# A decode block on one core: two heads a unit in three fixed 64 KB slots, without the tile framework

## The chip, the cores and the metric

The kernel runs on one core of one Trainium2 chip. The metric is the device time of one execution in microseconds (us). The kernel before was timed in three runs: 1331.37, 1329.55 and 1329.38 us, median 1329.55 us. Beside the timed runs, one execution was recorded by the hardware profiler; all rows quoted here come from that one.

The names of the engines: PE is TensorE (PEld its weight loads), DVE is VectorE, ACT is ScalarE, POOL is GpSimd, SP is the sequencer that issues nearly all DMA transfers. DMA stands for the core's 16 DMA engines, which share every large transfer.

## What is computed

One decode step of a transformer block for a batch of 2 rows, all in float32. The attention part has 32 heads with a cache of 8192 positions and 128 elements a head; the feed-forward part has 1792 hidden columns.

```python
# B, D = 2, 512;  H, Sk, Dh = 32, 8192, 128;  F = 1792
q = (layernorm(x) @ wq).reshape(B, 1, H, Dh)               # one query per row and head
scores = einsum("bhqd,bhkd->bhqk", q, k_cache) * Dh ** -0.5
p = softmax(scores)
o = einsum("bhqk,bhkd->bhqd", p, v_cache)
h = x + o.reshape(B, 1, H * Dh) @ wo
g = silu(layernorm(h) @ w_gate)
out = h + (g * (layernorm(h) @ w_up)) @ w_down
```

Each of the two caches has 64 pieces (2 rows x 32 heads) of 8192 x 128 floats, 4 MB a piece. Keys and values are 537 MB together, the five weight matrices 28 MB more. Every byte is used once, so all of it passes from HBM to SBUF once.

## The kernel before

The function `tile_decode_block` is written on the tile framework, with the order of the instructions given by hand (`manual_schedule`). Its unit of work is one (head, row) pair `i`, 64 of them. A piece of 4 MB lies in SBUF as 128 partitions x 32 KB: 64 positions of 128 elements on each partition.

**The ring.** All that is streamed (keys, values, wq and wo in four pieces of 2 MB each, w_gate, w_up, w_down) goes through one ring of five slots of 32 KB a partition (`RING = 5`, line 15; the pool on line 51). A list `order` (lines 80 to 99), made once, sets the order of the transfers: keys run ahead of values by up to four pairs (`LEAD`, `after`, lines 74 to 78). `pump()` (line 136) issues the next transfer on SP's queue as soon as the fifth item before it is marked used. The queue is one, so a transfer that waits for its slot holds all that stand behind it.

**The scores** (DVE). For each pair, `mult` (line 226) multiplies the keys in place by the query, which stands on every partition, and `reduce` (line 229) sums each position's 128 products. Both go in halves of 4096 elements a partition. `local_max` (line 237) takes each partition's maximum; a matmul against the identity (line 241) turns these 128 numbers into a row, DVE takes the row's maximum (line 245), and a matmul (line 247) spreads it to all partitions. ACT takes the exponentials with their sums (line 252), a matmul adds the sums up (line 256), DVE takes the reciprocal (line 260).

**The values** (PE). `pv` (line 262) makes 64 matmuls a pair: the weights are one column of the exponentials, the moving operand 128 positions' values of one column `j`, 128 columns wide. Four of PE's column groups are used in turn (`t = j % 4`), which puts four partial sums on partitions 0, 32, 64 and 96 of `opart`. `epilogue` (line 277) adds them up and divides.

**The projections.** `project_q` (line 197) has the query already copied to all partitions as its weights (128 columns wide), so its 16 matmuls for eight heads give a query that stands on all 128 partitions. It runs four times, before each group of eight heads. `project_o` (line 286) does the same grouping for wo. After the last value, lines 364 to 426 do the second layernorm, the gate and up projections (line 375), the transposes (line 394), the down projection (lines 406 and 421) with 512 columns, and the output.

## Time and profile before

| what | us |
|---|---|
| median of three runs | 1329.55 |
| span of the profiled execution | 1330.2 |
| DVE busy | 1156.7 |
| PE busy | 599.8 |
| ACT busy | 80.8 |

The span runs from the first instruction to the last on the slowest core (here the only one). No separate time is recorded for the profiled execution; its span is 0.65 us above the median of the timed runs. To read the page: "busy" is the time in which an engine has an instruction in work. The DMA share is the mean busy share of the 16 DMA engines, GB/s what they moved. The chain of waits starts at the last instruction and goes back at each step to what released it. PEclk is the clock that TensorE was granted, as a part of full speed: it moves between 0.50 and 1.00 in this trace.

### The profile page before, as it was taken

What the parts mean: (1) busy time and instruction counts of PE and PEld (TensorE: products, weight loads), DVE (VectorE), ACT (ScalarE), POOL (GpSimd) and SP (SyncE); (2) the same over time, 40 slices, a digit from 0 to 9 for tenths busy, and PEclk for the clock granted to TensorE, in tenths of its full rate; (3) what the DMA queues carried; (4) which work ended last, traced back from release to release, by engine and by line L of the source; (5) the groups of instructions that cost most, each with busy time, mean ns of one, the idle gap of its engine ahead of it and who ended that gap; (6) DMA issues with size and microseconds to landing.
All of it is one profiled execution on the core that took longest, in us unless ns stands there. A gap on an engine that the chain in (4) does not pass through costs nothing.

```text
span 1330.2 us, 19346 instructions
## 1 busy us (share of the span) xinstructions
PE 599.8 (45%) x9004; PEld 379.0 (28%) x9004; DVE 1156.7 (87%) x478; ACT 80.8 (6%) x341; POOL 1.9 (0%) x9
## 2 busy tenths in 40 slices
PE   5443432247443324425652443442644544244586
PEld 2322322134232213323321332232332223222341
DVE  6999999997899999988889999997799999999501
ACT  1000000001000000000100000000100000000010
POOL 0000000000000000000000000000000000000000
PEclk9656666568666666667776656665766875666687
DMA  9999999999999999999999999999999999999996
GB/s 410 425 440 426 432 433 430 431 433 435 428 430 434 429 437 429 433 432 431 433 428 429 437 428 438 427 428 437 425 438 392 428 436 427 437 429 437 428 417 266
DMA packets 28680, 565.91 MB, mean 425 GB/s; under 512 B 2484, under 2 KB 2484, under 8 KB 11448
## 3 DMA queue, kind: packets, MB, share of 16 engines
q1 hardware_dynamic: 28596, 564.67, 99.0%
q8 instruction: 70, 1.15, 0.3%
q14 instruction: 10, 0.08, 0.0%
q10 hardware_dynamic: 4, 0.00, 0.0%
HBM read 564.66 MB, written 0.00 MB: 425 GB/s over the span
## 4 chain that ended last, share of the span: by engine, by line
DMA 47%; DVE 45%; PE 7%; issue 0%; ACT 0%; SPq 0%; DVEq 0%; ACTq 0%
DMA ring<-in_A_k_cache_dram 34%; DVE s L229 22%; DVE ring L226 22%; DMA ring<-in_A_v_cache_dram 12%; PE wide L204 4%; PE opart L267 2%; DMA ring<-in_B_w_up_dram 1%; DMA ring<-in_A_wq_dram 1%; DVE m L237 0%; PE wide L406 0%; DVE r L260 0%; DVE gm L245 0%; PE small L241 0%; PE wide L375 0%; PE small L401 0%
## 5 line engine op out<-in xcount | busy, mean ns | idle before, releaser
L226 DVE TENSOR_TENSOR ring<-ring,qsb 128x4096 f32<-128x4096 f32 (+1 forms) x130 | 565.5, 4350 | 76.3 <-DMA ring<-in_A_k_cache_dram 61.5
L229 DVE TENSOR_REDUCE s<-ring 128x32 f32<-128x4096 f32 (+1 forms) x130 | 565.1, 4347 | 0.4 <-DVE gm L245 0.3
L267 PE MATMUL opart<-ring,p 128*1 128x128 f32 x8192 | 358.6, 357 | 120.4 <-DMA ring<-in_A_v_cache_dram 120.4
L267 PEld LDWEIGHTS opart<-ring,p 128*1 128x1 f32 x8192 | 250.4, 108 | 214.8 <-DMA ring<-in_A_v_cache_dram 125.4
L241 PE MATMUL small<-ident,m 128*1 128x128 f32 x128 | 31.1, 335 | 277.1 <-DVE m L237 277.1
L247 PE MATMUL small<-gm,nscale 1*128 1x1 f32 x128 | 35.8, 346 | 264.4 <-DVE gm L245 264.4
L247 PEld LDWEIGHTS small<-gm,nscale 1*128 1x128 f32 x128 | 30.3, 292 | 274.3 <-DVE gm L245 272.5
L241 PEld LDWEIGHTS small<-ident,m 128*1 128x1 f32 x128 | 5.5, 81 | 296.8 <-DVE m L237 294.5
L204 PE MATMUL wide<-ring,xb 128*128 128x512 f32 x128 | 58.6, 618 | 3.0 <-DMA ring<-in_A_wq_dram 3.0
L256 PE MATMUL small<-rs,ones 128*128 128x1 f32 x128 | 36.2, 352 | 46.9 <-ACT p L252 46.9
L245 DVE TENSOR_REDUCE gm<-small 1x1 f32<-1x128 f32 x64 | 17.4, 272 | 35.8 <-PE small L241 35.8
L280 ACT ACTIVATE osb<-opart 128x128 f32<-128x128 f32 x64 | 17.7, 277 | 494.4 <-PE opart L267 494.4
L256 PEld LDWEIGHTS small<-rs,ones 128*128 128x128 f32 x128 | 30.7, 298 | 52.4 <-ACT p L252 52.4
L204 PEld LDWEIGHTS wide<-ring,xb 128*128 128x128 f32 x128 | 25.0, 198 | 34.1 <-issue 34.1
L249 ACT ACTIVATE nb<-small 128x1 f32<-128x1 f32 x64 | 10.9, 171 | 375.1 <-PE small L247 374.7
L290 PE MATMUL attn<-ring,oT 128*2 128x512 f32 x64 | 33.0, 672 | 0.3 <-ACT oT L283 0.3
L282 PE MATMUL small<-r,osb 128*128 128x1 f32 x128 | 31.2, 313 | 4.2 <-ACT osb L280 4.2
L282 PEld LDWEIGHTS small<-r,osb 128*128 128x128 f32 x128 | 25.8, 251 | 24.9 <-issue 18.1
L283 ACT ACTIVATE oT<-small 128x1 f32<-128x1 f32 x64 | 11.0, 171 | 259.9 <-PE small L282 259.9
L365 DVE TENSOR_TENSOR h<-attn,xs 2x512 f32<-2x512 f32 x1 | 0.7, 679 | 29.0 <-PE attn L290 29.0
L252 ACT ACTIVATE p<-s,nb 128x64 f32<-128x64 f32 x64 | 22.3, 348 | 2.1
L237 DVE TENSOR_REDUCE m<-s 128x1 f32<-128x64 f32 x64 | 14.1, 220 | 2.2
(51 smaller groups left out, 79.4 us busy)
## 6 DMA issues: line engine op xcount, KB each, us to landing
ring<-in_A_k_cache_dram SPq DMA_DIRECT2D x63, 4096.0 KB, 32.0
ring<-in_A_v_cache_dram SPq DMA_DIRECT2D x63, 4096.0 KB, 30.6
ring<-in_A_wq_dram SPq DMA_DIRECT2D x4, 2048.0 KB, 25.6
ring<-in_A_wo_dram SPq DMA_DIRECT2D x4, 2048.0 KB, 28.3
ring<-in_A_k_cache_dram SPq DMA_DIRECT2D x4, 1024.0 KB, 11.1
ring<-in_A_v_cache_dram SPq DMA_DIRECT2D x4, 1024.0 KB, 24.9
ring<-in_B_w_gate_dram SPq DMA_DIRECT2D x4, 896.0 KB, 25.9
ring<-in_B_w_up_dram SPq DMA_DIRECT2D x4, 896.0 KB, 17.5
```

What stands on the lines that cost most here:

```text
L204: nc.tensor.matmul(ps, xb[:, c * B + b, :], w[:, c, n : n + 512], start=(c == 0), stop=(c == DC - 1),)
L226: nc.vector.tensor_tensor(kt, kt, qb, op=OP.mult)
L229: nc.vector.tensor_reduce(st[i]["s"][:, j0 : j0 + n], k_view(i, j0, n), axis=AX.X, op=OP.add)
L241: nc.tensor.matmul(st[i]["mrow"], st[i]["m"], ident, start=True, stop=True)
L245: nc.vector.tensor_reduce(gm, st[i]["mrow"], axis=AX.X, op=OP.max)
L247: nc.tensor.matmul(nb_ps, nscale, gm, start=True, stop=True)
L252: nc.scalar.activation(st[i]["p"], st[i]["s"], AF.Exp, bias=nb, scale=SCALE, accum_out=rs)
L256: nc.tensor.matmul(st[i]["den"], ones, rs, start=True, stop=True)
L267: nc.tensor.matmul(o[32 * t : 32 * t + 1, :], st[i]["p"][:, j : j + 1], vt[:, j, :], start=(j < 4), stop=(j >= NJ - 4),)
L280: nc.scalar.activation(osb, opart[i % 2], AF.Copy)
L282: nc.tensor.matmul(ot_ps, osb, st[i]["r"], start=True, stop=True)
L290: nc.tensor.matmul(attn, oT[:, h, :], w[:, h - g * G, :], start=(h == 0), stop=(h == H - 1))
```

## The change

The kernel is written anew without the tile framework: `decode_block` places every tensor at a fixed address and orders the engines by semaphores that it counts itself (`Count`, `take`). What it computes is the same. Its parts:

- **Units.** A unit is two neighbouring heads of one row; there are 32. Partitions 0 to 63 hold the first head, 64 to 127 the second, and each partition holds 128 positions (64 KB, one contiguous run in HBM). DVE's two large instructions cover a whole unit, 16384 elements a partition.
- **Slots.** Three slots of 64 KB a partition: A and B for keys in turn, C for values. wq is loaded whole (8 MB) into C before the first values, wo whole into A after the last keys there, w_gate and w_up into B, w_down into C.
- **Order on SP's queue.** After wq and the keys of units 0 and 1, values of unit u and keys of unit u + 2 alternate. Values wait until PE has finished the values before them (`s_pv`), keys until DVE has summed the keys that lie in their slot (`s_red`).
- **Values.** 32 matmuls a unit: the weights are 8 columns (4 positions x 2 heads, each head's column zero on the other head's partitions), the moving operand 512 columns. Only the matching blocks of the result are used: ACT copies all of it with the factor 1/sum, and four small matmuls (`gather`) pick out and add up the blocks.
- **The loop.** PE's work of units 0 to 30 is one loop (`Fori`) with one unit as its body: values(u), gather(u), softmax(u + 1). The other engines' instructions are unrolled.
- **Projections.** The query is projected in rows (32 weight columns, four column groups), then copied to the 64 partitions of its head by 32 small matmuls. wo's heads 0 to 29 go in four column groups, heads 30 and 31 after the last values. In the down projection the output is held in four groups of 128 columns on partitions 0, 32, 64 and 96 (`f4`), 13 of 14 row blocks go in two halves of 256 columns, and the result leaves in two DMAs.
- **Layouts.** wo and w_down come from the host arranged by partition; wq, w_gate and w_up are read with four neighbouring rows on a partition. So each transfer reads one contiguous run of 2 to 64 KB for each partition, where wo and w_down were read in runs of 2 KB before, and wq in runs of 4 KB.

```diff
-    ring = ctx.enter_context(tc.tile_pool(name="ring", bufs=RING))
...
+    A, BB, C = (BASE + s * SLOT for s in range(3))
+    ks = [arena("kA", A, [P, NJ, DH]), arena("kB", BB, [P, NJ, DH])]
+    vs = arena("vC", C, [P, NJ, DH])
+    wq_s = arena("wqC", C, [P, DC, H * DH])
+    wo_s = arena("woA", A, [P, H, D])
...
+    load(s["kB"], flat(ks[1], 0, NJ), kv_src(k_cache, 1))
+    for u in range(NU - 1):
+        if u == 0:
+            sp.wait_ge(s["pe"].h, 3)
+        else:
+            sp.wait_ge(s["pv"].h, u)
+        load(s["v"], flat(vs, 0, NJ), kv_src(v_cache, u))
+        if u + 2 < NU:
+            sp.wait_ge(s["red"].h, u + 1)
+            load(s["kB" if u % 2 else "kA"], flat(ks[u % 2], 0, NJ), kv_src(k_cache, u + 2))
+    sp.wait_ge(s["red"].h, NU - 1)
+    load(s["wo"], wo_s[:, :, :], wo)
+    sp.wait_ge(s["pv"].h, NU - 1)
+    cut = 96
+    load(s["v"], flat(vs, 0, cut), kv_src(v_cache, NU - 1)[:, : cut * DH])
+    load(s["v2"], flat(vs, cut, NJ), kv_src(v_cache, NU - 1)[:, cut * DH :])
+    sp.wait_ge(s["red"].h, NU)
+    load(s["g"], wg_s[:, :, :], w_gate.rearrange("(p c) f -> p c f", p=P))
...
+    load(s["u1"], wu_s[:, :3, :], up_src[:, :3, :])
+    load(s["u2"], wu_s[:, 3:, :], up_src[:, 3:, :])
+    sp.wait_ge(s["pv"].h, NU)
+    load(s["d1"], wd_s[:, : FB - 1, :], w_down[:, : FB - 1, :])
+    load(s["d2"], wd_s[:, FB - 1 :, :], w_down[:, FB - 1 :, :])
...
-        o = opart[i % 2]
-        for j in range(j0, j0 + n):
-            t = j % 4
-            nc.tensor.matmul(
-                o[32 * t : 32 * t + 1, :],
-                st[i]["p"][:, j : j + 1],
-                vt[:, j, :],
...
+    def values(g0, g1):
+        for g in range(g0, g1):
+            t = g % 4
+            ins = pe.matmul(
+                opart[32 * t : 32 * t + 8, :],
+                p2[:, 4 * g : 4 * g + 4, :].rearrange("p j b -> p (j b)"),
+                vs[:, 4 * g : 4 * g + 4, :].rearrange("p j d -> p (j d)"),
...
+    softmax()
+    with nc.Fori(0, NU - 1, engines=OrderedEngineSet([pe.engine]), head_slot={pe.engine: 0}):
+        take(pe, s["v"], 16)
+        values(0, NJ // 4).then_inc(s["pv"].h, 1)
+        gather()
+        softmax()
...
+            products(u, 0, NJ)
+            recip(u - 1)
+            wait(dve, "dve")
+            ins = sums(u, 0, NJ)
+        s["red"].on(ins)
...
+        s["mt"].on(dve.tensor_reduce(m_t[:, :], s_t[:, :], axis=AX.X, op=OP.max))
+        dve.wait_ge(s["mrow"].h, u + 1)
...
-    for k in range(grouped):
-        n, t = divmod(k, 4)
-        nc.tensor.matmul(
-            y_ps[32 * t : 32 * t + 32, :],
-            gT[:, n, 32 * t : 32 * t + 32],
-            w[:, k, :],
...
+    pe.wait_ge(s["d1"].h, 16)
+    last = FB - 1
+    for k in range(last):
+        g, t = divmod(k, 4)
+        for e, y in enumerate((attn4, wide1)):
+            ins = pe.matmul(
+                y[32 * t : 32 * t + 32, :256],
+                gT[:, g, 32 * t : 32 * t + 32],
+                wd_s[:, k, 256 * e : 256 * e + 256],
...
+    pe.wait_ge(s["d2"].h, 16)
+    for c in range(4):
+        ins = pe.matmul(
+            f4[32 * c : 32 * c + 2, :P],
+            gT[:, g, 32 * t : 32 * t + 2],
+            wd_s[:, last, c * P : (c + 1) * P],
...
+    for b, eng in ((0, sp), (1, act)):
```

SP's queue, where the stream begins and goes into its rhythm, before (`ring` is the five-slot ring; the shape is partitions x elements):

```order
L118 DMA ring<-in_A_wq_dram 128x4x1024
L113 DMA ring<-in_A_k_cache_dram 128x2048 x4
L113 DMA ring<-in_A_k_cache_dram 128x8192
L113 DMA ring<-in_A_v_cache_dram 128x8192
```

And the same place now, with the semaphore that each transfer waits for:

```order
L131 DMA wqC<-in_A_wq_dram 128x16384 [waits barrier_Pool_Activation_PE_DVE_SP_release]
L131 DMA kA<-in_A_k_cache_dram 128x8192 x2
L131 DMA kB<-in_A_k_cache_dram 128x16384
L131 DMA vC<-in_A_v_cache_dram 128x16384 [waits s_pe]
L131 DMA kA<-in_A_k_cache_dram 128x16384 [waits s_red]
L131 DMA vC<-in_A_v_cache_dram 128x16384 [waits s_pv]
L131 DMA kB<-in_A_k_cache_dram 128x16384 [waits s_red]
```

The whole wq stands ahead of the keys, a transfer is twice as long, and values have one slot that each transfer takes over from the one before.

PE, one pair before (two such groups make what is one unit now):

```order
L267 MATMUL opart_95<-ring,p 1x128 x64
L241 MATMUL small<-ident,m 1x128
L282 MATMUL small<-r,osb 128x1
L247 MATMUL small<-gm,nscale 128x1
L256 MATMUL small<-rs,ones 128x1
```

And the loop of the changed kernel (`vC` the values, `p` the weights, `sel` the picking matrix; line 426 is the loop's own branch):

```order
L408 MATMUL bank<-vC,p_69 8x512 x32
L420 MATMUL bank<-sel_64,osb 128x2 x4
L393 MATMUL bank<-ident,m 1x128
L397 MATMUL bank<-gm,nscale 128x2
L401 MATMUL bank<-rs,hm 128x1
L426 REGISTER_ALU
L426 COMPARE_AND_BRANCH
```

The 128 narrow matmuls of two pairs are 32 wide ones; the softmax of the next unit stands behind this unit's values and gather; and the rows stand once for 31 units.

DVE, one unit before (first half and second half of one pair) and now:

```order
L226 TENSOR_TENSOR ring<-ring,qsb 128x4096
L245 TENSOR_REDUCE gm<-small 1x1
L229 TENSOR_REDUCE s<-ring 128x32
L226 TENSOR_TENSOR ring<-ring,qsb 128x4096
L260 RECIPROCAL r<-small 128x1
L229 TENSOR_REDUCE s<-ring 128x32
L237 TENSOR_REDUCE m<-s 128x1
```

```order
L302 TENSOR_TENSOR kB<-kB,q_all 128x16384
L314 RECIPROCAL r<-bank 128x1
L308 TENSOR_REDUCE s<-kB 128x128
L337 TENSOR_REDUCE m<-s 128x1
L340 TENSOR_REDUCE gm<-bank 1x2
```

The row maximum (`gm`) was taken under cover of the next pair's products; now it stands right behind `m`, with PE's matmul between them, before the next unit's products.

More of the change, by code (lines that the diff above doesn't have):

```diff
@@ L36, in tile_decode_block @@
     F = w_gate.shape[1]
[L37 removed]
+    assert DH == P and B == 2 and D == 512 and F == 14 * P and H == 32 and S == 64 * P
     DC = D // P
@@ new lines, in decode_block @@
+    sg = late.new("sg", [P, 4, P])
+    gu = late.new("gu", [P, 4, P])
+    gT = late.new("gT", [P, 4, P])
+    ysb = late.new("ysb", [P, D])
+    res = late.new("res", [P, P])
+    banks = [nc.alloc_psum_tensor(f"bank{i}", [P, 512], F32) for i in range(8)]
+    opart, small1, small2, attn4, h_ps, wide0, wide1, f4 = banks
+    names = (
+        "x wq k0 k0b kA kB v v2 wo g u1 u2 d1 d2 o1 o2 "
+        "dve act pool pe red pv ot mrow nbp den mt gmt rst osbt r oTt"
+    ).split()
+    s = {n: Count(nc, f"s_{n}") for n in names}
@@ new lines, in decode_block, with softmax @@
+    for u in range(NU):
+        weights(u)
+        if u < NU - 1:
+            outputs(u)
+    act.activation(warm[:, :], mhalf[:1, :], AF.Sigmoid)
+    def softmax():
+        take(pe, s["mt"])
+        pe.matmul(small1[0:1, :P], m_t[:, :], ident[:, :], start=True, stop=True).then_inc(
+            s["mrow"].h, 1
+        )
+        take(pe, s["gmt"])
+        pe.matmul(small1[:, 264:266], nscale[:, :], gm[:, :], start=True, stop=True).then_inc(
+            s["nbp"].h, 1
+        )
+        take(pe, s["rst"])
+        pe.matmul(small1[:, 256:257], hm[:, :], rs[:, :], start=True, stop=True).then_inc(
+            s["den"].h, 1
+        )
@@ new lines, in values, with gather @@
+    def values(g0, g1):
[5 more added lines that the diff above has]
+                vs[:, 4 * g : 4 * g + 4, :].rearrange("p j d -> p (j d)"),
+                start=(g < 4),
+                stop=(g >= NJ // 4 - 4),
+            )
+        return ins
+    def gather():
+        take(pe, s["osbt"])
+        for j in range(4):
+            ins = pe.matmul(
+                small2[:, 16:18], osb[:, j, :], sel8[:, j, :], start=(j == 0), stop=(j == 3)
+            )
+        ins.then_inc(s["ot"].h, 1)
@@ new lines, in decode_block @@
+    n = s["pe"].on(ins)
+    act.wait_ge(s["pe"].h, n)
+    act.wait_ge(s["red"].h, NU)
+    n = s["act"].on(act.activation(attn_s[:, :], attn4[:, :], AF.Copy))
+    pe.matmul(h_ps[:B, :], ident[:B, :B], xs[:, :], start=True, stop=False)
+    pe.wait_ge(s["act"].h, n)
+    pe.matmul(h_ps[:B, :], sel8[:, 0, :], attn_s[:, :], start=False, stop=False)
+    take(pe, s["v"], 16)
+    values(0, cut // 4)
+    pe.wait_ge(s["v2"].h, 16)
+    values(cut // 4, NJ // 4).then_inc(s["pv"].h, 1)
+    outputs(NU - 1)
```

726 lines of the change are left out of this document (393 added, 333 removed).

## The prediction

> **What bounds the kernel now.** I read the page's head and its DMA part first.
>
> ```profile
> span 1330.2 us, 19346 instructions
> PE 599.8 (45%) x9004; PEld 379.0 (28%) x9004; DVE 1156.7 (87%) x478; ACT 80.8 (6%) x341; POOL 1.9 (0%) x9
> ...
> DMA packets 28680, 565.91 MB, mean 425 GB/s; under 512 B 2484, under 2 KB 2484, under 8 KB 11448
> ...
> q1 hardware_dynamic: 28596, 564.67, 99.0%
> q8 instruction: 70, 1.15, 0.3%
> ```
>
> DVE is busy 87% of the span, the DMA engines 99%. Second I read the busy time by stretches, to see where the stream is not full (the columns end with PE's clock, the DMA share and GB/s).
>
> ```profile
> 0.00:5.00 5.00, 0.54 (x4) 0.50 (x4) 2.13 (x9) 1.28 (x1) 1.39 (x8) 1.00 0.63 224
> 50.00:1000.00 950.00, 409.19 (x6272) 267.11 (x6272) 876.82 (x344) 56.98 (x249) 0.00 (x0) 0.65 1.00 432
> 1000.00:1050.00 50.00, 26.28 (x295) 13.32 (x295) 49.90 (x20) 2.90 (x14) 0.00 (x0) 0.69 0.96 405
> 1250.00:1300.00 50.00, 38.05 (x672) 23.02 (x672) 0.81 (x3) 4.34 (x15) 0.00 (x0) 0.77 1.00 418
> 1315.00:1320.00 5.00, 4.18 (x16) 1.10 (x18) 1.38 (x2) 0.00 (x0) 0.00 (x0) 0.50 0.62 240
> 1320.00:1325.00 5.00, 5.00 (x26) 0.90 (x18) 0.42 (x1) 0.15 (x1) 0.00 (x0) 0.59 0.13 51
> 1325.00:1330.00 5.00, 2.04 (x5) 0.26 (x4) 0.68 (x1) 0.23 (x1) 0.00 (x0) 1.00 0.00 1
> ```
>
> So the kernel is bound by its transfers: from 50 to 1000 us the share is 1.00 at 432 GB/s. The stream was short of work once (1000 to 1050 us, 405 GB/s, which is 27 x 50 / 432 = 3.1 us) and slower where the pieces are small (1250 to 1300 us, 418 GB/s, 1.6 us). At 1315 us there were 240 x 5 + 51 x 5 = 1.5 MB left, 3.4 us' worth, so the stream's end is about 1318.4, though some engines still worked after 1320: the sixteen don't end together. Third, the chain and the waits of SP's queue:
>
> ```profile
> DMA 47%; DVE 45%; PE 7%; issue 0%; ACT 0%; SPq 0%; DVEq 0%; ACTq 0%
> ...
> SPq L113 <- DVE m L237: 953.1, 60, 18.4
> ```
>
> The chain gives DVE 45%, because SP waits most for keys to be used up (953.1 us). That is no second bound: while SP waits, older transfers fill the engines. What can be won is only what the stream loses, and what lies ahead of and behind it.
>
> **The change part by part.** First the stream itself. Its rate with 64 KB runs isn't in the trace, so I take it from the length of a run. Around 344 us a piece of wo passes, in runs of 2 KB:
>
> ```profile
> 342.00:346.00 4.00, 0.82 (x4) 0.74 (x4) 4.00 (x3) 0.61 (x3) 0.00 (x0) 0.50 1.00 401
> ```
>
> At 401 GB/s over 16 engines a run of 2 KB takes 81.7 ns of one engine; at 432 GB/s a run of 32 KB takes 1213.6 ns. The difference for 30 KB is 1131.9 ns, so 64 KB take 1213.6 + 32/30 x 1131.9 = 2421 ns, which is 433.1 GB/s. Ends: 432 if nothing is saved, and 434.4 if the refills of instructions (0.3%, below) go as well. I take 433.1, because it uses only the rows on length. Keys, values, wq and wo are 66 transfers of 8.389 MB, 553.7 MB: 1278.3 us (ends 1281.6 and 1274.5). The rest, 11.0 MB in runs of 28, 21, 7, 26 and 2 KB, costs by the same line 8 x (1062.6 + 798.5 + 270.3 + 987.2 + 81.7 ns) = 25.6 us. Ahead of it: the first 5 us moved 224 GB/s, 2.6 us' worth, so 2.4 us are lost. The last piece lands at 2.4 + 1278.3 + 25.6 = 1306.3 us, the 13 blocks of w_down ahead of it 0.65 us sooner, 1305.7. Against 1318.4 this is 12 us: 3.1 the empty stretch, 3.3 the longer runs, the rest the small pieces and the last weights.
>
> This holds if no transfer is issued late. A transfer of 8.389 MB takes 19.4 us, a unit 38.7 us. Three engines must keep to that.
>
> *Values' slot (PE, SP).* The new wait that matters: values u + 1 can't be issued before PE has used values u; behind it on SP's queue stand the keys of unit u + 3. Cover is one transfer of keys, 19.4 us.
>
> ```profile
> L267 PE MATMUL opart<-ring,p 128*1 128x128 f32 x8192 | 358.6, 357 | 120.4 <-DMA ring<-in_A_v_cache_dram 120.4
> L406 PE MATMUL wide<-ring,gT 128*32 128x512 f32 x24 | 5.3, 1048 | 0.0
> 0.73 0.54 ACTq L57 DMA_DIRECT2D xs<-in_A_x_dram  x1
> 2.15 0.68 DVE L172 BATCH_NORM_STATS2 ln_stats<-xs 2x6 f32<-2x512 f32 x1 [0.63 <-DMA xs<-in_A_x_dram]
> ```
>
> A matmul is two records. A unit streams as many columns as before (64 records of 512 for 256 of 128): 358.6 / 32 = 11.2 us. The nearest rows in form, four column groups with 512 columns, take 5.3 / 24 = 0.22 us a record at a clock of 0.50 to 0.59, so 64 x 0.22 = 14.0 us. Ends: 7.0 us (that at clock 1.00) and 14.0; I take 12, nearer the row of the same work. From issue to the data's use passed 1.4 us for x (0.73 to 2.15). So 12 + 1.4 = 13.4 of 19.4 us, 6.0 us spare, 4.0 at the bad end. Cost nothing, hidden by the keys' transfer.
>
> *Keys' slots (DVE).* DVE's large instructions by length:
>
> ```profile
> 28.62 2.28 DVE L226 TENSOR_TENSOR ring<-ring,qsb 128x2048 f32<-128x2048 f32 x1
> 33.26 0.22 DVE L237 TENSOR_REDUCE m<-s 128x1 f32<-128x64 f32 x1
> 33.40 4.42 DVE L226 TENSOR_TENSOR ring<-ring,qsb 128x4096 f32<-128x4096 f32 x1
> 33.54 0.58 PE L241 MATMUL small<-ident,m 128*1 128x128 f32 x2 [8.85 <-DVE m L237]
> 37.73 0.27 DVE L245 TENSOR_REDUCE gm<-small 1x1 f32<-1x128 f32 x1
> 46.59 0.15 DVE L260 RECIPROCAL r<-small 128x1 f32<-128x1 f32 x1
> ```
>
> 2048 elements more cost 2.14 us, so 16384 take 4.42 + 6 x 2.14 = 17.3 us, two of them 34.5. With the reciprocal 0.15, the maximum of 128 columns (0.22 + 0.07), PE's matmul that now stands uncovered between the two maxima (0.58 and some 0.3 of handing over) and 0.27, a unit is 36.1 us, where two pairs took 8 x 4.4 + 1.3 = 36.6. Below 38.7: DVE waits for keys, 2.6 us a unit. Keys of unit u + 2 have their turn 58.1 us after keys of u landed (values, keys, values), and the slot is free after 36.1: 22 us spare. At the other end DVE could be up to 2.6 us a unit slower at no cost.
>
> *PE's row ahead of DVE.* The softmax of unit u + 1 stands behind values u, whose data land 19.4 us after the keys of u + 1. With 12 us and some 3 us of gather PE is free at 34.4 us, DVE's maximum comes at 34.9. With 14.0 us DVE would wait 1.5 us, which its 2.6 us hold.
>
> *Start.* DVE's first products started at 15.05 us; now all of wq lands first.
>
> ```profile
> 8.09 16.60 PE L204 MATMUL wide<-ring,xb 128*128 128x512 f32 x32 [3.04 <-DMA ring<-in_A_wq_dram]
> 15.05 2.29 DVE L226 TENSOR_TENSOR ring<-ring,qsb 128x2048 f32<-128x2048 f32 x1 [9.07 <-ACT qsb L211]
> ```
>
> wq lands at 2.4 + 19.4 = 21.8 us. The projection's 64 records at 16.60 / 32 = 0.52 us (one after another there, four groups here) take 8.3 us, copies and spreading some 2: 32 us, when the first half of the keys has come (31.5). DVE ends unit 0 at 68 us; its slot's turn is at 2.4 + 4 x 19.4 = 80. So 17 us of later start cost nothing, and 12 us more would be covered. For the stream values 0 wait for the projection (31 us, turn at 60).
>
> *The tail.* Its matmuls before, and the steps around them:
>
> ```profile
> 1299.64 0.68 DVE L365 TENSOR_TENSOR h<-attn,xs 2x512 f32<-2x512 f32 x1 [28.96 <-PE attn L290]
> 1303.37 7.05 PE L375 MATMUL wide<-ring,hT 128*32 128x512 f32 x48 [0.31 <-issue]
> 1315.46 0.69 DVE L391 TENSOR_TENSOR gu<-wide,sg 128x512 f32<-128x512 f32 x1 [5.38 <-PE wide L375]
> 1319.04 5.27 PE L406 MATMUL wide<-ring,gT 128*32 128x512 f32 x24
> 1325.28 1.02 PE L420 MATMUL small<-ysb,pick 128*2 128x512 f32 x2
> 1327.20 0.68 DVE L425 COPY res<-small 2x512 f32<-2x512 f32 x1 [2.39 <-PE small L421]
> ```
>
> The last values land at 2.4 + 1278.3 = 1280.7. Their remaining 16 records (2.6 us), copy, gather, two rows of wo (some 4.5) and the layernorm (1299.64 to 1303.37, 3.7) end at 1291.5; the gate by 1296.5, the up projection after its last piece (1297.9) by 1300; gu to gT (1315.46 to 1319.04, 3.6) by 1304. So w_down's landing at 1305.7 sets the end. From there: 52 records of half the columns, 5.7 us at clock 0.50 to 0.59 and 2.9 at 1.00, I take 4.3; copies 0.45; the four groups of 128 columns twice 0.4 (1.02 / 4 and its latency) in place of two times about 1; the copy of 128 columns 0.2; and 2.3 from there to the span's end as before (1327.88 to 1330.2). Sum 8.1 us, where 1318.4 to 1330.2 were 11.8. Span 1305.7 + 8.1 = 1313.8; less the 0.65 us by which the span lies over the median: 1313 us. Two small surcharges (6 or so refills, 0.4, and the wait for the slowest engine, 0.5) make it 1314.
>
> *Instructions.* 70 refills took 0.3% of the engines, 4.0 us on each, and 19346 / 70 = 276 instructions make one. The program now has some 258 matmuls of four instructions in the text; with the other engines about a twelfth of before. No run here shows a backward branch. [...]
>
> **The rivals.**
>
> *The loop fetches its body again each time* (0.11). For: the body is 39 matmuls, about 160 instructions, up to two refills, 31 times. Against: it is under one refill's 276. The wait hides, since PE idles some 20 us before values land. The transfers don't: 62 refills of 0.3% x 1330 x 16 / 70 = 0.9 us are 3.5 us on the mean engine, up to 7 on the worst. 1318 to 1321 us.
>
> *PE's tail at half clock* (0.07). For: the clock is 0.50 at 1315 to 1320 us. Then the chain from the last values is late: 1280.7 + 8.5 + 3.7 + 6.1 + 6.1 + 4.4 = 1309.5, then 5.7 + 3.8: 1319 us. Against: the clock was 0.77 from 1250 to 1300 us.
>
> *The values' slot comes late and the stream runs dry in each unit* (0.07). Slower. For: one slot for values where the ring had five, and engines that end unevenly, by some 5 us at 1315 to 1325 us. 14.0 + 1.4 + 5 = 20.4 us, 1.0 over the cover, 31 times: 1345 us. It decides from 0.5 us a unit on. Against: an engine that is behind is behind once, not in each unit.
>
> *Runs of 64 KB are slower* (0.04). No row has them; at 425 GB/s the stream is 24 us longer: 1338 us. Against: the rate rose with length.
>
> *DVE becomes the pace* (0.03): at 39.5 us a unit it ends at 31.5 + 32 x 39.5 = 1295.5; w_gate waits for its slot, then 1.4 + 25.6 + 7.4: 1330, no change.
>
> **How the numbers follow.** The forecast, 1314 us, has 0.68; its own bounds are 1309 (434.4 GB/s, 3.8 us, and full clock, 1.4) to 1319 (432 GB/s, half clock). The first two rivals reach 1321, with both together 1327. Range 1308 to 1327: left out are the slower cases (0.11), the unchanged one and a little below. 0.2% (2.7 us) is what can be told from no change: faster 0.86 (forecast and first two rivals), same 0.03, slower 0.11.
>
> **What would show it.** Right: a DMA share of 1.00 at 433 GB/s from 50 to 1300 us, DVE idle on keys some 2.6 us a unit, SP's wait for PE ending 4 to 6 us before the keys' transfer does, few refills. Wrong: a share below 1.00 in each unit with SP waiting on the values' matmuls, a values group over 18 us, or the last chain running through PE from 1281 us on.

## The result and the profile after

The changed kernel takes **1314.09 us** (median of 4 runs, 1313.86 to 1314.24); the kernel before, measured beside it, 1329.49 (1329.38 to 1331.37). The ratio is 0.988, with a 95% interval of 0.9866 to 0.9894: 15.4 us or 1.2% less. The profiled execution has a span of 1312.3 us and took 1314.05 us. The prediction said 1314.

The page's head and its DMA part, of the kernel after:

```profile
span 1312.3 us, 6527 instructions
PE 425.3 (32%) x2844; PEld 142.8 (11%) x2844; DVE 1130.5 (86%) x191; ACT 75.7 (6%) x242; POOL 1.8 (0%) x8
...
DMA packets 10540, 564.77 MB, mean 430 GB/s; under 512 B 1178, under 2 KB 1186, under 8 KB 1444
...
q1 hardware_dynamic: 10520, 564.66, 99.4%
q8 instruction: 4, 0.07, 0.0%
```

The bytes are the same, in 10540 packets where there were 28680. PE's queue of instructions (q8) was refilled 4 times where it was 70. DVE is busy for 86% of the span, where it was 87%, and the DMA engines for 99.4%, where it was 99.0%: the bound has not moved.

The busy time by stretches, after (columns as in the prediction: length, PE, PEld, DVE, ACT, POOL, PE's clock, DMA share, GB/s):

```profile
0.00:5.00 5.00, 0.00 (x0) 0.00 (x0) 3.06 (x13) 1.28 (x1) 1.22 (x7) 1.00 0.79 302
50.00:1000.00 950.00, 287.53 (x1878) 96.37 (x1878) 870.49 (x126) 49.48 (x173) 0.00 (x0) 0.61 1.00 434
1000.00:1050.00 50.00, 13.74 (x90) 4.42 (x94) 46.45 (x8) 2.01 (x7) 0.00 (x0) 0.60 1.02 440
1250.00:1300.00 50.00, 35.27 (x215) 10.38 (x212) 10.23 (x12) 6.14 (x14) 0.54 (x1) 0.80 0.99 427
1300.00:1305.00 5.00, 2.94 (x28) 0.90 (x22) 1.12 (x2) 0.38 (x1) 0.00 (x0) 1.00 0.72 302
1305.00:1310.00 5.00, 4.23 (x68) 2.79 (x68) 0.52 (x2) 0.38 (x1) 0.00 (x0) 1.00 0.00 1
```

Read it against the same rows of before. The stretch with an empty queue (1000 to 1050 us, 405 GB/s) has gone. The small pieces from 1250 us on run at 427 GB/s instead of 418. The stream now stops sharply: next to nothing (1 GB/s) moves after 1305, where before 51 GB/s still trickled at 1320 to 1325. And it ends some 13.5 us sooner (about 1304.9 against the 1318.4 that the prediction worked out for before). From there to the end of the span it is 7.4 us, where it was 11.8. The two together, 17.9 us, are all of the difference between the spans, 1330.2 and 1312.3.

One unit of the loop, as the timeline of the kernel after shows it (start, duration, engine, line and operation, in brackets the idle time ahead and what ended it), with the start and the tail:

```profile
22.67 9.10 PE L261 MATMUL bank<-wqC,xT 128*32 128x512 f32 x64 [16.38 <-DMA wqC<-in_A_wq_dram]
34.34 8.69 DVE L302 TENSOR_TENSOR kA<-kA,q_all 128x8192 f32<-128x8192 f32 x1 [27.40 <-ACT q_all L291]
...
603.51 17.23 DVE L302 TENSOR_TENSOR kB<-kB,q_all 128x16384 f32<-128x16384 f32 x1 [2.83 <-DMA kB<-in_A_k_cache_dram]
622.91 9.33 PE L408 MATMUL bank<-vC,p 128*8 128x512 f32 x64 [19.59 <-PEq L121]
632.30 0.33 SPq L131 DMA_DIRECT2D vC<-in_A_v_cache_dram  x1
642.18 17.23 DVE L302 TENSOR_TENSOR kA<-kA,q_all 128x16384 f32<-128x16384 f32 x1 [2.82 <-DMA kA<-in_A_k_cache_dram]
...
1305.04 3.61 PE L535 MATMUL bank<-wdC,gT 128*32 128x256 f32 x52 [1.27 <-DMA wdC<-in_B_w_down_dram]
```

A unit is 642.18 - 603.51 = 38.67 us. DVE waits 2.8 us in it for its keys: the transfers set the pace, not DVE. PE has used the values at 632.24, and SP issues the next ones at 632.30. The keys whose transfer covers this are used from 642.18 on, so 9.9 us of cover were left. In the tail PE waited 1.27 us for w_down.

From the chain that ended last, in order of time, after:

```profile
1275.32 8.79 PE bank L408 x64
...
1284.12 20.79 DMA wdC<-in_B_w_down_dram
...
1305.04 3.63 PE bank L535 x52
```

It runs from the last values, which free the slot, through the landing of w_down's blocks (1304.91), as the prediction had it, and not through PE's own work from the last values on.

And the groups of instructions by line, after, for the two engines that have to keep up:

```profile
L408 PE MATMUL bank<-vC,p 128*8 128x512 f32 x2048 | 291.8, 734 | 584.9 <-PEq L121 584.9
L302 DVE TENSOR_TENSOR kB<-kB,q_all 128x16384 f32<-128x16384 f32 x16 | 275.6, 17223 | 39.6 <-DMA kB<-in_A_k_cache_dram 39.6
```

Values take 291.8 / 32 = 9.1 us a unit, and DVE's large instructions wait for keys only.

### The profile page after: what moved, and what is told of

Same layout as the page of the kernel before. It is cut to its first block, busy times and chain, and to the rows that moved or that the text cites. A ratio compares the mean times of both kernels' runs of the same rounds, so it can differ in the third digit from the quotient of the medians.

```text
span 1312.3 us, 6527 instructions
## 1 busy us (share of the span) xinstructions
PE 425.3 (32%) x2844; PEld 142.8 (11%) x2844; DVE 1130.5 (86%) x191; ACT 75.7 (6%) x242; POOL 1.8 (0%) x8
## 2 busy tenths in 40 slices
DMA packets 10540, 564.77 MB, mean 430 GB/s; under 512 B 1178, under 2 KB 1186, under 8 KB 1444
## 3 DMA queue, kind: packets, MB, share of 16 engines
q1 hardware_dynamic: 10520, 564.66, 99.4%
## 5 line engine op out<-in xcount | busy, mean ns | idle before, releaser
L408 PE MATMUL bank<-vC,p 128*8 128x512 f32 x2048 | 291.8, 734 | 584.9 <-PEq L121 584.9
L302 DVE TENSOR_TENSOR kA<-kA,q_all 128x16384 f32<-128x16384 f32 (+1 forms) x17 | 275.7, 16220 | 64.3 <-DMA kA<-in_A_k_cache_dram 36.9
L302 DVE TENSOR_TENSOR kB<-kB,q_all 128x16384 f32<-128x16384 f32 x16 | 275.6, 17223 | 39.6 <-DMA kB<-in_A_k_cache_dram 39.6
L308 DVE TENSOR_REDUCE s<-kA 128x128 f32<-128x16384 f32 (+1 forms) x17 | 275.7, 16216 | 0.1
L308 DVE TENSOR_REDUCE s<-kB 128x128 f32<-128x16384 f32 x16 | 275.5, 17220 | 0.0
L408 PEld LDWEIGHTS bank<-vC,p 128*8 128x8 f32 x2048 | 60.5, 103 | 790.1 <-issue 790.1
L393 PE MATMUL bank<-ident,m 128*1 128x128 f32 x64 | 18.7, 395 | 182.9 <-PEq L121 182.9
L371 ACT ACTIVATE osb<-bank,r 128x512 f32<-128x512 f32 x32 | 22.0, 687 | 902.0 <-PE bank L408 902.0
L420 PE MATMUL bank<-sel,osb 128*128 128x2 f32 x256 | 32.8, 250 | 29.0 <-PEq L121 29.0
L420 PEld LDWEIGHTS bank<-sel,osb 128*128 128x128 f32 x256 | 31.0, 191 | 57.7 <-issue 57.7
L401 PE MATMUL bank<-rs,hm 128*128 128x1 f32 x64 | 17.9, 348 | 44.1 <-PEq L121 44.1
L356 ACT ACTIVATE p<-s,nb 64x128 f32<-64x128 f32 x64 | 25.9, 405 | 1.4
L397 PE MATMUL bank<-gm,nscale 1*128 1x2 f32 x64 | 17.6, 343 | 14.8 <-PEq L121 14.8
L356 ACT ACTIVATION_READ_ACCUMULATOR p<-s,nb 64x1 f32 x64 | 11.8, 185 | 0.0
```

The lines of the kernel that those rows point to most:

```text
L302: dve.tensor_tensor(kt, kt, q_all[:, u, :][:, None, :].to_broadcast([P, n, DH]), op=OP.mult)
L308: return dve.tensor_reduce(s_t[:, j0 : j0 + n], ks[u % 2][:, j0 : j0 + n, :], axis=AX.X, op=OP.add)
L356: ins = act.activation(p2[a:z, :, e], s_t[a:z, :], AF.Exp, bias=nb[a:z, e : e + 1], scale=SCALE, accum_out=rs[a:z, :],)
L371: act.activation(osb[:, :, :].rearrange("p j d -> p (j d)"), opart[:, :], AF.Copy, scale=r_t[:, :],)
L393: pe.matmul(small1[0:1, :P], m_t[:, :], ident[:, :], start=True, stop=True).then_inc(s["mrow"].h, 1)
L397: pe.matmul(small1[:, 264:266], nscale[:, :], gm[:, :], start=True, stop=True).then_inc(s["nbp"].h, 1)
```

## The experiments

Theory A is that of the prediction: transfers bound the kernel; the gain is longer runs, no empty stretch, fewer refills and a shorter tail; values and DVE are covered and could be slower at no cost. Against it stood that values or DVE are close to setting the pace, and that refills or the shape of the matmuls matter by themselves. "More" and "less" are against the 1314.09 of the changed kernel. Not all runs are of one chip; the kernel before took 1329.49 to 1330.28 us on them (medians), so a difference of 1 us isn't settled.

### Runs of 32 KB

```diff
-    load(s["kB"], flat(ks[1], 0, NJ), kv_src(k_cache, 1))
+    load2(s["kB"], ks[1], kv_src(k_cache, 1))   # two transfers, half the columns each
...                                              # wq, wo, keys and values alike
```

> Changed kernel, but every transfer of 64 KB runs is issued as two transfers of 32 KB runs to the same slot. Theory (a longer run saves a fixed cost of some 6 ns each, worked out from 401 GB/s at 2 KB and 432 GB/s at 32 KB): 66 transfers take 1281.6 us in place of 1278.3, so 1314.1 + 3.3 = 1317.4 us and 432 GB/s from 50 to 1000 us. Rival (the stream gained by the refills that are gone, the length of a run is nothing): 1314 us, within 1 us, and the rate stays at 434 GB/s.

1317.37 us (1316.4 to 1318.52), ratio 0.9901 (0.9887 to 0.9916): 3.3 us more. Of the busy time by stretches, the row of the steady stream:

```profile
50.00:1000.00 950.00, 285.68 (x1878) 96.17 (x1878) 867.60 (x126) 49.49 (x173) 0.00 (x0) 0.61 1.00 433
```

The stream is slower by 1 GB/s of 434. Of the timeline of the same run, w_down's blocks in the tail:

```profile
1307.77 5.30 PE L543 MATMUL bank<-wdC,gT 128*32 128x256 f32 x52 [2.86 <-DMA wdC<-in_B_w_down_dram]
```

The total agrees with theory A, but the traces divide it in another way. PE's last block starts at 1307.77 instead of 1305.04, 2.7 us later, and 0.6 of that was lost in the first 5 us (250 GB/s instead of 302). So the length of the runs is worth 2.1 to 2.7 us. The records of the single packets agree: half of all packets of 64 KB in the changed kernel take 2418 ns or less, half of those of 32 KB here 1213 ns or less, so two of them are 8 ns longer than one. The rest is the tail: the same 52 records took 5.30 us instead of 3.61. PE had idled 2.86 us ahead of them and ran at half clock (0.50 from 1310 to 1312 us); after an idle 1.27 us it had kept full clock. So the agreement of the total with the expectation is partly chance.

### The loop written out, and the old width of the matmuls

Three kernels share this question: does the gain need the loop, the wide matmuls, or both?

```diff
# e2: written out
-    with nc.Fori(0, NU - 1, engines=OrderedEngineSet([pe.engine]), head_slot={pe.engine: 0}):
+    for _ in range(NU - 1):
# e4: narrow matmuls, in the loop
-                opart[32 * t : 32 * t + 8, :],
-                p2[:, 4 * g : 4 * g + 4, :].rearrange("p j b -> p (j b)"),
-                vs[:, 4 * g : 4 * g + 4, :].rearrange("p j d -> p (j d)"),
+                opart[32 * t : 32 * t + 2, :P],
+                p2[:, j, :],
+                vs[:, j, :],
# e3: both
```

> Changed kernel with PE's loop written out 31 times. About 30 x 165 = 5000 more instructions, at 276 a refill 18 more refills. Theory (a refill takes one DMA engine 0.9 us, and the stream goes by the engines that take them): 18 x 0.9 / 16 = 1.0 us if they spread over all engines, 2 us if over half of them: 1315 to 1316 us. Rival (the loop's branch and its bookkeeping cost something each time round): under 1313 us. Rival (refills are hidden): 1314 us. [...]

1316.96 us (1316.67 to 1319.59), ratio 0.9905 (0.9891 to 0.992), 2.9 us more. Of the DMA part of its page, PE's refills:

```profile
q8 instruction: 23, 0.38, 0.1%
```

And of its timeline, w_down's blocks:

```profile
1308.08 3.64 PE L535 MATMUL bank<-wdC,gT 128*32 128x256 f32 x52 [0.19 <-DVE gT L516]
```

There are 19 refills more, where 18 had been worked out. wo's matmuls start on their data at 1263.18 instead of 1260.71, so the stream was 2.5 us late there. PE's chain was so late behind it that it, and no longer w_down, sets the end (`<-DVE gT`).

> The narrow matmuls of the run before inside the loop: its body is some 550 instructions, two refills' worth or more. If the loop's body is fetched again each time round: 62 or more refills in the page's row, 1317.6 to 1321 us as with the loop written out. If PE keeps the body: the 4 refills of the changed kernel and 1314 us, whatever the width. The time between the written-out and the looped one is then the cost of refills alone, at the same work. [...]

1316.37 us (1316.01 to 1316.72), ratio 0.9896 (0.9881 to 0.991), 2.3 us more. Of the DMA part of its page, PE's refills:

```profile
q8 instruction: 7, 0.11, 0.0%
```

Of its groups by line, the values:

```profile
L408 PE MATMUL bank<-vC,p 128*2 128x128 f32 x8192 | 292.7, 315 | 593.2 <-PEq L121 589.2 <-issue 4.0
```

Of its timeline, w_down's blocks:

```profile
1305.46 5.30 PE L535 MATMUL bank<-wdC,gT 128*32 128x256 f32 x52 [2.57 <-DMA wdC<-in_B_w_down_dram]
```

The body of this loop has some 550 instructions, twice what one refill brings (276, by 19346 instructions and 70 refills of the kernel before), and 7 refills in all say that it isn't fetched again in 31 rounds. Its values take 292.7 / 32 = 9.1 us, as the wide ones do: four matmuls of 128 columns stand for one of 512 without cost. w_down lands 0.4 us later than in the changed kernel; the other 1.7 us are again the half clock in the tail, after an idle 2.57 us. So the wide form by itself is worth nothing that shows here.

> As the one with the loop written out, and the values' matmuls 128 columns wide with 2 weight columns, 128 a unit in place of 32 (gather then needs one matmul in place of four). About 31 x 550 = 17000 instructions, 62 refills, near the 70 of the kernel before. Theory (refills delay the stream): 62 x 0.9 / 16 = 3.5 us if spread over all engines, 7 us if over half: 1317.6 to 1321 us, and the values' matmuls take about 11 us a unit where they take 9.1. Rival (refills are hidden, the gain came from run length and the tail): 1314 us. Rival (PE's longer group empties the queue): a DMA share below 1.00 in each unit and over 1325 us.

1333.31 us (1331.49 to 1336.51), ratio 1.0029 (1.0019 to 1.0039): 19 us more than the changed kernel, and slower than the kernel before. The expectation was far too low. Of the DMA part of its page, PE's refills:

```profile
q8 instruction: 69, 1.13, 0.3%
```

Of its groups by line, the values, with the idle time that PE spent on instructions (`issue`):

```profile
L408 PE MATMUL bank<-vC,p 128*2 128x128 f32 x8192 | 316.0, 324 | 660.8 <-PEq L121 595.7 <-issue 65.1
```

Of its timeline, one group of values:

```profile
393.67 5.97 PE L408 MATMUL bank<-vC,p 128*2 128x128 f32 x126 [20.31 <-PEq L121]
401.55 3.67 PE L408 MATMUL bank<-vC,p 128*2 128x128 f32 x128 [1.92 <-issue]
408.57 0.52 PE L408 MATMUL bank<-vC,p 128*2 128x128 f32 x2 [3.34 <-issue]
409.12 0.33 SPq L131 DMA_DIRECT2D vC<-in_A_v_cache_dram  x1
```

The work of PE is that of the narrow loop, so 17 us go with the 62 refills. PE stops inside the values for its next instructions (1.92 and 3.34 us here, 65.1 in all, where the narrow matmuls in the loop had 4.0); the group lasts 393.67 to 409.09, 15.4 us, instead of 9. That alone would still fit under 19.4 us of keys, yet units of 40 to 41.7 us appear. The landings in the trace point to the transfers themselves: from the landing of values to that of the next keys are 19.76 us on the mean, where the changed kernel has 19.33, and from keys to values 19.45, where it has 19.32. Over 30 units this is 13 us in the keys' transfers and 4 in those of values, and values that are issued late would lengthen their own first. So most of the 17 us seem to be the refills' work on the transfer engines, and not PE's waits; no run isolates it.

### Values two and three times

Extra passes of the same matmuls into a bank that isn't read lengthen the values.

```diff
         take(pe, s["v"], 16)
+        for _ in range(n - 1):            # n = 2, 3
+            for g in range(NJ // 4):
+                pe.matmul(wide0[...], p2[...], vs[...], ...)
         values(0, NJ // 4).then_inc(s["pv"].h, 1)
```

> Changed kernel, with each unit's values' matmuls of the loop done once more into a bank that nobody reads, ahead of the real ones (more work, same output). At full clock 64 records of 512 columns are 6.8 us. In the changed kernel's trace values end 9.3 us after they land and the next values are issued at 632.30 us, while the keys that cover them land at 642.2: less some 1.5 us from issue to data, 8.4 us are spare. Theory (the one values' slot costs nothing while it is covered): 6.8 of 8.4 us are used up, 1314 us, at most 2 us more. Rival (the slot already sets the pace in some units): 31 x 6.8 = 211 us more, 1525 us, or a good part of it.

1335.6 us (1330.66 to 1341.7), ratio 1.0049 (1.0027 to 1.007): 21.5 us more where no cost was expected. The groups by line (L431 is the extra pass):

```profile
L431 PE MATMUL bank<-vC,p 128*8 128x512 f32 x1984 | 283.1, 735 | 545.2 <-PEq L121 545.2
L408 PE MATMUL bank<-vC,p 128*8 128x512 f32 x2048 | 225.4, 592 | 2.2 <-PEq L121 2.2
```

Values now take 283.1 / 31 + 225.4 / 32 = 16.2 us. With the 1.4 us that the prediction took for a transfer's start this is 17.6 of 19.4. It should have been covered, and it wasn't. (The profiled execution was the shortest of the eight, 1330.66 us.) Another path could have done it: the softmax of the next unit stands behind the values on PE, so DVE's maximum now comes later. The waits of SP's queue speak against it:

```profile
SPq L131 <- PE bank L408: 1189.2, 32, 40.5
SPq L131 <- DVE s L308: 47.3, 4, 36.9
```

Before 32 transfers SP waits for PE's values, and only before 4 for DVE's sums (32 in the changed kernel). PE, too, starts each group 0.14 us after its values have landed, so the softmax isn't late for it.

> The same with two more passes, 13.6 us. Theory: 13.6 - 8.4 = 5.2 us beyond the cover in each of 31 units, 161 us: 1475 us, with a DMA share near 0.88 and SP waiting on the values' matmuls. If the keys behind them in SP's queue move along and something else covers: 1314 us. It gives the point from which the values' slot decides.

1495.66 us (1494.09 to 1497.24), ratio 1.1242 (1.1208 to 1.1275). Past the cover in every unit, and 20 us more than expected. Of its busy time by stretches, the steady stream:

```profile
50.00:1000.00 950.00, 517.47 (x4332) 144.57 (x4332) 756.18 (x111) 43.45 (x152) 0.00 (x0) 0.76 0.89 378
```

Of its timeline, PE's values (L431 the extra passes) and the issue of the next ones:

```profile
617.60 15.46 PE L431 MATMUL bank<-vC,p 128*8 128x512 f32 x128 [17.25 <-PEq L121]
...
632.88 7.04 PE L408 MATMUL bank<-vC,p 128*8 128x512 f32 x64
...
639.99 0.33 SPq L131 DMA_DIRECT2D vC<-in_A_v_cache_dram  x1
...
661.92 15.49 PE L431 MATMUL bank<-vC,p 128*8 128x512 f32 x128 [17.21 <-PEq L121]
```

Here a share of 0.89 shows the rival of the prediction at work, the stream running dry in each unit. It also prices the wait: from the issue at 639.99 to the data's use at 661.92 are 21.9 us, some 19.4 of them the transfer at full rate, so **2.5 us** pass between the issue and a stream that runs again. The prediction had 1.4, from a load of 4 KB at the start. With 2.5 the doubled values need 16.2 + 2.5 = 18.7 of 19.4 us, and 0.7 us is what the sixteen engines may end apart. In the records of the changed kernel's transfers they end 1.4 to 1.9 us apart, in those of the doubled run 0.5 to 3.4. This explains the doubled case by its size; no run took only that difference away. The loss is not the same in each unit: in 13 of 30 units of the doubled run the next values land 38.6 or 38.7 us later, as in the changed kernel, in the worst 41.7 us. With tripled values the sum is 22.5 + 2.5 + 19.4 = 44.4 us, which is the unit measured (661.92 - 617.60 = 44.3).

### DVE slower by 2.2 and by 4.5 us a unit

One or two extra reductions of 2048 elements in each unit, whose result isn't used:

```diff
             recip(u - 1)
+            for i in range(n):            # n = 1, 2
+                V(dve.tensor_reduce(extra[:, i, :], ks[u % 2][:, :16, :], axis=AX.X, op=OP.add))
             ins = sums(u, 0, NJ)
```

> Changed kernel, with one more reduction of 2048 elements a partition in each unit on DVE, into a scratch column that nobody reads: 2.2 us a unit, where DVE waits 2.8 us a unit for keys. Theory (the stream is the bound, DVE has room): 1314 us. Rival (DVE and the stream share the span, as the chain of the kernel before put 45% on DVE): 31 x 2.2 = 69 us more, 1383 us, or half of it.

1316.2 us (1317.05 and 1315.35), ratio 0.9893 (0.9864 to 0.9922): 2.1 us more, not 69 more. Of its busy time by stretches, the steady stream:

```profile
50.00:1000.00 950.00, 286.49 (x1878) 96.26 (x1878) 922.02 (x150) 49.47 (x173) 0.00 (x0) 0.61 1.00 434
```

Of its timeline, w_down's blocks:

```profile
1305.27 6.52 PE L540 MATMUL bank<-wdC,gT 128*32 128x256 f32 x52 [4.54 <-DMA wdC<-in_B_w_down_dram]
```

DVE did 67 us more work and the stream lost nothing: 434 GB/s, w_down used from 1305.27 instead of 1305.04. That DVE bounds the kernel is refuted, although it is busy 91% now. The 3.0 us by which this execution's span is longer (1315.3 against 1312.3) are the tail's clock: 6.52 us for the 52 records, at 0.50, after an idle 4.54 us.

> Two such reductions, 4.5 us a unit: DVE needs 35.9 + 4.5 = 40.4 us a unit, over the stream's 38.7. Theory: DVE is now the pace. It starts at 34.3 us, ends its 32 units at 34 + 32 x 40.4 = 1327 us; w_gate waits for DVE's slot, so 1.4 + 25.6 + 7.2 us follow: 1361 us. Rival (slots soak it up): 1314 us.

1364.12 us (1363.71 and 1364.53), ratio 1.0253 (1.0223 to 1.0283). DVE's 35.8 + 4.5 us are over the 38.7 of the transfers, and now DVE is the pace, as expected to 3 us. Of its busy time by stretches, the steady stream:

```profile
50.00:1000.00 950.00, 291.76 (x1820) 108.10 (x1824) 930.67 (x167) 47.44 (x166) 0.00 (x0) 0.61 0.99 423
```

A unit takes 40.1 us, and DVE's wait for keys, 76.5 us in all in the changed kernel and 11.4 with one reduction, is gone. So the spare time of DVE lies between 2.2 and 4.5 us, as its wait of 2.8 us says. Note that the share of the DMA engines alone (0.99) would hardly have told this.

### Output in rows

The down projection and output as before: 512 columns, two output partitions, one output transfer.

```diff
-        for e, y in enumerate((attn4, wide1)):
-            ins = pe.matmul(y[32 * t : 32 * t + 32, :256], ..., wd_s[:, k, 256 * e : 256 * e + 256], ...)
+        ins = pe.matmul(attn4[32 * t : 32 * t + 32, :], ..., wd_s[:, k, :], ...)
...
-    for b, eng in ((0, sp), (1, act)):
+    s["o1"].on(sp.dma_start(out.rearrange("b s d -> (b s) d"), res2[:, :]), 16)
```

> Changed kernel with the down projection and the output as in the kernel before: 512 columns, the output on two partitions, the two copies of the partial sums one after the other, one output transfer. Theory (the tail's own work counts in full behind the last landing): 12 blocks in four groups of 512 columns 3.3 us at full clock (3.6 now), copies 0.85 (0.45), three blocks of two records of 512 at 0.43 us each, one of them hidden, 1.7 to 2.6 (0.7), copy of 512 columns 0.68 (0.29): 2 to 2.8 us more, 1316 to 1317 us. Rival (the output's landing hides it, or two transfers cost more than one): 1314 us or less.

1316.08 us (1314.54 to 1316.82), ratio 0.9891 (0.9876 to 0.9906): 2.0 us more, the lower end of what was expected. Part of it is the clock again, as the timeline shows: 24 records at 128x512 took 4.48 us after an idle 2.33 us.

```profile
1305.65 4.48 PE L527 MATMUL bank<-wdC,gT 128*32 128x512 f32 x24 [2.33 <-DMA wdC<-in_B_w_down_dram]
```

They stream 12288 columns; at the rate of the changed kernel (13312 columns in 3.61 us) this is 3.3 us, so 1.1 of the 2.0 is not the form of the output.

### w_down in three pieces

```diff
-    load(s["d1"], wd_s[:, : FB - 1, :], w_down[:, : FB - 1, :])
+    load(s["d1"], wd_s[:, :8, :], w_down[:, :8, :])
+    load(s["k0"], wd_s[:, 8 : FB - 1, :], w_down[:, 8 : FB - 1, :])
```

> Changed kernel with w_down in three transfers, 8, 5 and 1 blocks, in place of 13 and 1, so that PE's first 32 records needn't wait for the 13th block. In the changed kernel gT is ready at 1303.9 us and the 13 blocks land at 1305.0; the first 8 would land 1.5 us sooner. Theory: the 2.2 us of the first 8 blocks begin at 1303.9, and after the last landing 1.4 us remain: 1 us less, 1313 us. Rival (another transfer's end costs as much as it saves): 1314 us.

1313.14 us (1312.15 to 1313.78), ratio 0.987 (0.9855 to 0.9885), the fastest of all; its interval overlaps that of the changed kernel, and it ran on another chip, so the 1.0 us isn't settled; in the traces the blocks begin 0.36 us sooner. Of its timeline, w_down's blocks:

```profile
1304.68 3.64 PE L538 MATMUL bank<-wdC,gT 128*32 128x256 f32 x52 [0.19 <-DVE gT L517]
```

PE no longer waits for weights, but for gT: PE's chain and the transfers end within half a microsecond of each other, and little is left to win from either alone.

### The kernel before with wo and w_down laid out by partition

```diff
-                wo[i * G * DH : (i + 1) * G * DH, :].rearrange("(c p) m -> p c m", p=P),
+                wo[:, i * G : (i + 1) * G, :],
-                w_down[e * P : (e + n) * P, :].rearrange("(c p) m -> p c m", p=P),
+                w_down[:, e : e + n, :],
```

> Kernel before, with one part of the change alone: wo and w_down arranged by partition, so they are read in runs of 16 KB and 2 to 8 KB in place of 2 KB. Theory (the short runs cost 81.7 ns for 2 KB where 16 KB take 610): wo's 4096 runs of one engine in 16 were 20.9 us, now 19.5; w_down's 9.2, now 8.5: 2 us less, 1327.5 us. Rival (the stream's losses are the empty stretch and the refills alone): 1329.5 us.

1329.15 us (1327.76 to 1330.23), ratio 0.999 (0.9981 to 0.9999): 0.75 us less than the kernel before on that chip (1329.9), not 2. Of its busy time by stretches, the one in which the queue is empty:

```profile
1000.00:1050.00 50.00, 26.49 (x296) 13.52 (x296) 49.90 (x20) 2.91 (x14) 0.00 (x0) 0.70 0.95 405
```

The stretch with the empty queue stays at 405 GB/s. So the layout, one part of the change that can be had alone, gives a twentieth of the gain; the rest isn't in it.

### Refills on GpSimd alone

To separate what refills cost the stream from what they cost PE, GpSimd executes 16000 extra memsets of one element between the layernorms, which nobody waits for.

```diff
+    for i in range(40):
+        for j in range(400):
+            ins = pool.memset(pad[:, j : j + 1], 0.0)
+        k = s["pad"].on(ins)
+        pool.wait_ge(s["pad"].h, k)
```

> Changed kernel, and on GpSimd, which has nothing to do between the two layernorms, 16000 memsets of one element: more instructions to fetch, and nobody waits for them (extra work, same output). At 276 instructions a refill these are 58 refills, as many as the narrow matmuls written out had (69, and 1333.3 us), without PE waiting for its own. Theory A (a refill takes one DMA engine some 0.93 us, only half of the engines take them, and the slowest engine sets the landings): 58 x 0.93 / 8 = 6.7 us more, 1321 us; then some 10 of the 19 us of the written-out narrow run are PE's own waits (65 us of idle time on fetches inside its values) that make the one values' slot come late. Theory B (all 19 us are the engines' time): 1330 us or more. Rival (refills cost nothing, all 19 us are PE's waits): 1314 us. If GpSimd's memsets take over 0.08 us each they run past the second layernorm and the run says nothing.

1397.95 us (1396.16 to 1398.78), ratio 1.0505 (1.0491 to 1.052): 84 us more, and no theory had it. Of the DMA part of its page, GpSimd's refills:

```profile
q14 instruction: 129, 1.06, 0.2%
```

Of the waits of GpSimd, that for instructions (us in total, times, longest):

```profile
POOL pad L230 <- issue: 147.8, 123, 3.5
```

Of the busy time by stretches, one while the memsets run (5 to 691 us) and one after them:

```profile
300.00:650.00 350.00, 92.86 (x624) 31.27 (x624) 279.17 (x41) 16.10 (x56) 273.57 (x8169) 0.60 0.91 384
750.00:1200.00 450.00, 136.63 (x892) 46.14 (x880) 405.06 (x59) 24.15 (x84) 0.00 (x0) 0.60 1.00 430
```

These are refills of another kind: 1.06 MB in 129, 8 KB each, on their own queue (q14), one for 128 memsets. They move 0.2% of the engines' time, yet the stream falls to 384 GB/s at a share of 0.91, and recovers when they end. A unit takes 43.9 us (DVE's products start at 287.87 and 331.77) instead of 38.7. Some 16 units at 5.2 us more are the 84 us. The share tells that some engines were idle, not that all were slowed. Of the timeline, one unit while the memsets run:

```profile
287.87 17.23 DVE L308 TENSOR_TENSOR kA<-kA,q_all 128x16384 f32<-128x16384 f32 x1 [8.26 <-DMA kA<-in_A_k_cache_dram]
...
309.93 8.87 PE L414 MATMUL bank<-vC,p 128*8 128x512 f32 x64 [27.69 <-PEq L122]
...
331.77 17.23 DVE L308 TENSOR_TENSOR kB<-kB,q_all 128x16384 f32<-128x16384 f32 x1 [8.26 <-DMA kB<-in_A_k_cache_dram]
```

DVE and PE start here when their data land. Values land 22.1 us after the keys and keys 21.8 us after the values, where the changed kernel has 19.4 and 19.3. So both transfers are longer by about the same, and the one slot for values isn't the cause: a late issue would lengthen the values' alone. The records of the single packets show what is. A refill comes every 5.49 us, and by the times of the packets all of them stand between the packets of one and the same of the sixteen engines. There a refill takes 0.31 us, the packet of 64 KB behind it 2.77 us instead of 2.42, the next one 2.42 again. An engine has 16 such packets in a unit, so this one needs 8 x 5.49 = 43.9 us, the unit that was measured, and the others wait for it (the sixteen end a transfer of values up to 14 us apart). What is 0.2% of all engines' time is 12% of this engine's while the memsets run. Theory A had the mechanism, a slowest engine that sets the landings, but spread the refills over eight engines.

## Why the prediction was right, and where it wasn't

**Direction and mechanism** were right: transfers bound the kernel, nothing was issued late, and the gain came where it was put. *Stream:* 433.1 GB/s was forecast, 434 measured. The first 5 us lost (434 - 302) x 5 / 434 = 1.5 us where 2.4 had been taken over from before. w_down's blocks were forecast to land at 1305.7 plus up to 0.9 of surcharges; they landed at 1304.9. The surcharge for refills and slow engines was not needed.

**Values' slot:** 12 us taken (7 to 14), 9.1 measured. 12 stood too near the slow end: within a group PE's clock climbs, from 0.50 to 1.00 (weights are loaded every 0.85 us at first, every 0.43 us later), so a group lies between the two ends. The start of a transfer, 1.4 us, was the wrong row: 2.5 in the run with tripled values. Together 11.6 instead of 13.4 of 19.4 us, so the conclusion held, but the margin was misread: cover ends at 16.9 us of values less the spread of the engines, not at 18.

**DVE:** a unit of 36.1 us forecast, 35.8 measured; its wait for keys 2.6 forecast, 2.8 measured; period 38.7 in both. The runs with 2.2 and 4.5 us more confirm the slack from both sides.

**Start:** wq 21.8 forecast, 22.67 in use; projection 8.3 us forecast, 9.10 measured; DVE's products 32 forecast, 34.34 measured. It cost nothing, as said.

**Tail:** gT was expected at 1304 and was there at 1303.9. From landing to the span's end 8.1 us forecast, 7.4 measured, because the 52 records took 3.6 us, not 4.3. The choice between full and half clock was left as a mean of two ends that no single run takes: a run has 3.6 or 5.3 to 6.5.

**The rival of half clock** (0.07) had the wrong mechanism. It let the chain from the last values be late; what the runs show is a wait that is too long ahead of the last block. Four experiments were 1 to 3 us slower for it, though the changed kernel itself kept the clock. **Fetching the body each time** (0.11) is refuted by 4 refills. **The values' slot late in each unit** (0.07) didn't occur in the changed kernel. Its argument against ("an engine that is behind is behind once, not in each unit") holds where little is missing: the doubled values lost nothing in 13 of 30 units. It does not where the work itself passes the cover (the tripled values, 5.7 us in each unit), nor where one engine is behind by new work in each unit (the refills on GpSimd, 5.2 us). **Slower long runs** (0.04) and **DVE as the pace** (0.03) are refuted by 434 GB/s and 2.8 us of waiting.

**The step that failed** is the last one, "less the 0.65 us by which the span lies over the median". The span of one execution was compared with the median of others. A run's time lies over its own span: 1314.05 over 1312.3 in the kernel after, and in all the runs by 1.2 to 1.9 us. So the profiled execution of before, with 1330.2, can only be the one that took 1331.37 us, the slowest of its runs. The offset should have been about +1.5, not -0.65. The sum for the span was 1313.8 + 0.9 = 1314.7 and so 2.4 us too long (0.9 of surcharges, 0.8 of landing, 0.7 of tail). Two errors of over 2 us cancelled. With the right offset the same working would have said 1316: the forecast was good to 0.2%, not to 0.01%.

**Where the 15.4 us come from:** 2.1 to 2.7 us are the longer runs; 2.0 the form of the output with the clock behind it; some 3 the stretch with the empty queue, by the windows; 0.75 the layouts, as far as before can have them. No run isolates the rest, about half, which by the traces is the sharp end of the stream (1305 against a trickle to after 1320) and the start. The loop and the wide matmuls aren't gains by themselves: to give up either costs 2 to 3 us, to give up both costs more than the whole gain (1333.31).

## What to carry to other kernels

With the stream full, count the rest of the cover of a slot that is used once at a time: the next transfer's time, less the work, less the start of a transfer, 2.5 us here. A rest of 7.8 us cost nothing, one of 0.7 us cost 13 us in the trace, and one of -5.6 us cost 5.7 us in each unit. Keep the instruction text of a saturated kernel short: a loop cost nothing here (4 refills for 31 rounds), refills cost far more than their bytes (62 on PE went with 17 us, where their queue held 0.3% of the engines' time). Ask of a transfer which of the engines ends last, and not only how busy all are on the mean (with the refills on GpSimd up to 14 us apart, at a mean share of 0.91). And compare a forecast span with spans, and a time with times.
